# A one-core decode kernel: the second weight of its gated MLP dealt anew over the DMA engines, its first product laid out to match, four fills moved

## The chip, the cores and the metric

The kernel runs on one core of a Trainium2 chip. A core has TensorE (PE), VectorE (DVE), ScalarE (ACT), GpSimd (POOL), SyncE (SP), which here only issues transfers, and sixteen DMA engines that carry every transfer. The metric is the device time of one execution in microseconds. All times inside an execution are counted from the start of the span that the profile shows.

## The reference

Two blocks work on the same four rows (batch 4, one position, 640 columns); their results and the input are added. Block A is attention over a cache, 32 heads of 128 with 4096 positions for each row; block B is a gated MLP whose spatial matrix is 1 x 1.

```python
xn = layernorm(x)                                    # (4, 640)
q  = xn @ wq                                         # (4, 32 heads, 128)
o  = softmax(q @ k_cache^T * 128**-0.5) @ v_cache    # caches: (4, 32, 4096, 128) each
z  = gelu(xn @ w_in)                                 # (4, 1728)
g  = w_sp * layernorm(z[:, 864:]) + b_sp
out = x + o @ wo + (z[:, :864] * g) @ w_out          # w_out: (864, 640)
```

The two caches are 134 MB each in bf16; everything else together is about 14 MB.

## The kernel before, in words

**The stream.** The caches are read in 16 units of keys (K0 to K15) and 16 of values (V0 to V15). A unit is one row of the batch and eight heads, 8.4 MB, with 65,536 bytes for each of the 128 partitions. SP issues every unit (L187) in the order K0, K1, K2, K3, V0, K4, V1, K5 and so on, and at the end the output weight `wo` (L195) in ever smaller parts. The units live in the tile `kv`, five slots of half a unit each. A load is issued only when its two slots are free: K0 goes to slots 3 and 4, K1 to 0 and 1, K2 to 2 and 3, so K2 waits until the first half of K0 has been read, and until block B is done with slot 2.

**A unit of keys.** DVE transposes it in eight steps (L419, into the first part of the tile `w_words`), and PE multiplies each step with the queries (L430). After four units DVE, ACT and POOL do the softmax (L437 to L486), and the next four units of values are multiplied (L501).

**Block B, before the first unit is used.** ACT loads `x` (L120), SP loads `wq` and `w_in` (L126, L129). DVE and POOL normalise `x` (L211 to L228), PE multiplies with `wq` (L299) and with `w_in` (L328), ACT applies gelu (L339, L342), DVE, POOL and ACT do the second layernorm and the gate (L365 to L384), and PE multiplies the result with `w_out` (L397, 52 products into `proj`). Only then may DVE's first transposes begin: `w_out` lies in `w_words`, where the transposed keys go.

**How `w_out` is laid out.** It is held as 128 partitions by 26 columns of 640 numbers. Its 864 rows of 1,280 bytes fill only some partitions, and DVE first fills the tile with zeros (L131). The rows come in pieces; the table `PC` gives for each piece its partitions (first, end, step), first column, number of columns `n`, the number `k` of groups into which the outermost dimension of the source is cut, and the run of rows that one packet takes. Two pieces (`a`, `b`) are issued by SP, four (`w`, `s`, `n`, `l`) by POOL, in that order, all after DVE's fill. A piece does not go over sixteen DMA engines but over few of them:

```python
in_=B_w_out[f_of[t][0]:f_of[t][1], :].rearrange("(r i c) n -> i r (c n)", i=k, c=run)
```

Four further small loads on SP (`marks`, L144) go into a tile that nothing reads.

**Rows of the gate.** The columns of `w_in` follow the rows of `w_out`, so each piece has its own part of the product with `w_in` and its own gelu instructions, which put the results where `w_out` expects them. Before, a piece whose rows are interleaved needs two to six of them.

**Order of the work.** Each engine runs its instructions in the order in which they stand in its queue. A scheduler sets that order for the part ahead of the first unit. On POOL it is: fills and the identities, the four loads of `w_out` (waiting for DVE's fill), `sq` (L217, the squares for the first layernorm), `I4` (L241), the selection matrices, and later block B's gate.

Of the kernel before, what the change touches and what calls it, by code (L numbers as in the profile page):

```python
# [8 lines left out]
ACT = mybir.ActivationFunctionType  # L9
# [3 lines left out]
BF16 = mybir.dt.bfloat16  # L13
# [3 lines left out]
def kernel(  # L17
# [19 lines left out]
    nc = tc.nc  # L37
    P = 128
    B, Sq, D = A_x.shape
    _, H, Sk, Dh = A_k_cache.shape  # L40
    assert Sq == 1 and B == 4 and Dh == P and D % P == 0
    DC = D // P
# [15 lines left out]

    PC = {"w": (0, 28, 2, 0, 9, 7, 9), "a": (32, 52, 1, 0, 10, 5, 10), "n": (68, 92, 2, 0, 8, 6, 8),
          "l": (92, 95, 1, 0, 26, 2, 13), "b": (1, 12, 2, 0, 26, 3, 26), "s": (60, 68, 1, 0, 26, 2, 26)}
    f_of, f_end = {}, 0
    for t, (p0, p1, st, _, n, _, _) in PC.items():
        f_of[t] = (f_end, f_end + len(range(p0, p1, st)) * n)
# [6 lines left out]
    eps = 1e-5  # L72

    const = ctx.enter_context(tc.tile_pool(name="const", bufs=1))
# [12 lines left out]
    def misc_ps(shape, dtype):  # L87
        misc_ctr[0] += 1
        return ps_m.tile(shape, dtype, tag="misc", name=f"misc{misc_ctr[0]}")
# [16 lines left out]
    def at_slot(i, n, off=0):  # L106
        return kv[:, i * SL + off:i * SL + off + n]
# [26 lines left out]
    def load_piece(eng, t):  # L134
        p0, p1, st, c0, n, k, run = PC[t]
        return eng.dma_start(out=w_out[p0:p1:st, c0:c0 + n].rearrange("p c n -> p (c n)"),
                             in_=B_w_out[f_of[t][0]:f_of[t][1], :].rearrange("(r i c) n -> i r (c n)", i=k, c=run))

    load_piece(nc.sync, "a")
    load_piece(nc.sync, "b")  # L140
    marks = const.tile([14, 288], BF16)
    m0 = 0
    for k, m in ((6, 96), (10, 80), (12, 64), (14, 48)):
        nc.sync.dma_start(out=marks[0:k, m0:m0 + m], in_=B_w_out[0:k, 0:m])  # L144
        m0 += m
    sw = load_piece(nc.gpsimd, "w")
    for t in ("s", "n", "l"):
        with tc.issue_after(sw.ins):
            sw = load_piece(nc.gpsimd, t)

# [51 lines left out]
    ident_f = const.tile([P, P], F32)  # L202
    make_identity(nc, ident_f[:])
    ones_f = const.tile([P, P], F32)
    nc.gpsimd.memset(ones_f[:], 1.0)
    eps_t = const.tile([P, 1], F32)
    nc.gpsimd.memset(eps_t[:], eps)

    lnb = ln_t[:XR, D:7 * D].bitcast(F32)
    xf, xc, sq = lnb[:, 0:D], lnb[:, D:2 * D], lnb[:, 2 * D:3 * D]  # L210
# [15 lines left out]
    xnT = const.tile([P, DC, 32], BF16)  # L226
# [17 lines left out]
    i2 = I32[:].rearrange("p (pr c) -> p c pr", c=C2)  # L244
    nc.gpsimd.tensor_tensor(out=SelP[:], in0=i2[:, 0], in1=i2[:, 1], op=ALU.add)
    SelN = const.tile([P, NE, HP * B], F32)
    nc.gpsimd.memset(SelN[:].rearrange("p e x -> p (e x)"), 0.0)
    for q in range(4):
        nc.gpsimd.tensor_scalar(out=SelN[32 * q:32 * q + 32, q % 2], in0=SelP[32 * q:32 * q + 32, :], scalar1=-scale,
                                scalar2=None, op0=ALU.mult)  # L250
# [19 lines left out]
    for q in range(4):  # L270
        nc.gpsimd.tensor_copy(out=SelE[32 * q:32 * q + 32, :, q % 2, :],
                              in_=b8[32 * q:32 * q + 32, 8:8 + HP, None].to_broadcast((32, HP, P // HG)))
# [10 lines left out]
                          in_=ident_f[:].rearrange("p (q x c) -> p q x c", q=2, c=C2))  # L283
# [4 lines left out]
    for hf in range(NH):  # L288
        nc.tensor.matmul(proj[0:32, 0:NO2], lhsT=ident_bf[:XR, 1 - hf:33 - hf],
                         rhs=x_bf[:, hf * NO2:(hf + 1) * NO2], start=(hf == 0), stop=False)  # L290
# [4 lines left out]
    for hf in range(2):  # L295
        for c in range(DC):
            for j in range(NG):
                n0 = j * HG * Dh + hf * 512
                nc.tensor.matmul(q4_ps[32 * j:32 * j + 32, hf * 512:hf * 512 + 512], lhsT=xnT[:, c, :],  # L299
                                 rhs=wq[:, c, n0:n0 + 512], start=(c == 0), stop=(c == DC - 1))  # L300
# [4 lines left out]
    for a in range(2):  # L305
# [9 lines left out]
    w_z = w_in.rearrange("p c (a f) -> p c a f", a=2)  # L315
    zr_ps = [misc_ps([P, 2, 256], F32) for _ in range(2)]


    z_parts = [(0, 0, w_z[:, :, :, f_of["w"][0]:f_of["w"][1]]), (0, 1, w_z[:, :, :, f_of["a"][0]:f_of["a"][1]]),
               (0, 2, w_z[:, :, :, f_of["n"][0]:f_of["l"][1]]), (1, 0, w_z[:, :, :, f_of["b"][0]:f_of["b"][1]])]  # L320
    s_src = w_z[:, :, :, f_of["s"][0]:f_of["s"][1]].rearrange("p d a (r i c) -> p d i a r c", i=2, c=PC["s"][4])
    z_parts += [(1, 1 + i, s_src[:, :, i]) for i in range(2)]
    for c in range(DC):
        for bk, q, src in z_parts:
            w = 1
            for m in src.shape[3:]:
                w *= m
            nc.tensor.matmul(zr_ps[bk][32 * q:32 * q + 32, :, 0:w], lhsT=xnT[:, c, :], rhs=src[:, c],  # L328
                             start=(c == 0), stop=(c == DC - 1))
    z_f = at_slot(2, 2 * 3 * NB, z_at).bitcast(F32).rearrange("p (a n) -> p a n", a=3)  # L330
    z_b = [ppool.tile([P, NB], BF16, tag="p", name=f"z_b{i}") for i in range(2)]
    zT = z_f[:, 0:2, :].rearrange("p a (i j) -> p a i j", j=32)
    nc.gpsimd.memset(z_f[:, 0:2, :], 0.0)
    def gelu(q, bk, f0, c0, n, x, order=None):

        z = zr_ps[bk][32 * q:32 * q + 32, :, f0:f0 + len(range(*x)) * n]
        dst = zT[32 * q:32 * q + 32, :, c0:c0 + n, x[0]:x[1]:x[2]]
        if order is None:
            nc.scalar.activation(out=dst, in_=z.rearrange("p a (x c) -> p a c x", c=n), func=ACT.Gelu_apprx_tanh)  # L339
        else:  # L340
            for a in range(2):
                nc.scalar.activation(out=dst[:, a].rearrange("p c (i r) -> p c i r", i=order),  # L342
                                     in_=z[:, a].rearrange("p (r i c) -> p c i r", i=order, c=n), func=ACT.Gelu_apprx_tanh)

    gelu(0, 0, 0, 0, 9, (0, 28, 2), 7)
    gelu(1, 0, 0, 0, 10, (0, 20, 1), 5)
    gelu(2, 0, 0, 0, 8, (4, 28, 2), 6)
    f_l = f_of["l"][0] - f_of["n"][0]
    for i in range(2):
        for j in range(3):  # L350
            x = 28 + (3 * i + j) // 2
            gelu(2, 0, f_l + 26 * j + 13 * i, 13 * ((3 * i + j) % 2), 13, (x, x + 1, 1))
    gelu(0, 1, 0, 0, 26, (1, 12, 2), 3)
    gelu(1, 1, 0, 0, 26, (28, 32, 1))
    gelu(2, 1, 0, 0, 26, (0, 4, 1))

    one_bf = const.tile([1, P], BF16)
    nc.gpsimd.memset(one_bf[:], 1.0)
    sb_ps = misc_ps([P, 2], F32)
    nc.tensor.matmul(sb_ps[:], lhsT=one_bf[:], rhs=sb_bf[:], start=True, stop=True)  # L360
    sb_f = const.tile([P, 2], F32)
# [30 lines left out]
    for f0 in range(0, FC, 4):  # L392
        for hf in range(NH):
            for fc in range(f0, min(f0 + 4, FC)):
# [3 lines left out]
                                 rhs=w_out[:, fc, hf * NO2:(hf + 1) * NO2],  # L398
                                 start=(fc == 1 and hf == 0), stop=False)
# [158 lines left out]
    for i, item in enumerate(seq):  # L558
# [10 lines left out]
        g, b = divmod(u, B)  # L569
# [22 lines left out]
    for c, hf in ((0, 0), (1, 0), (0, 1), (1, 1), (2, 0), (2, 1)):  # L592
        p = min(c, 1)
# [49 lines left out]
```

## Time and profile before

| what | us |
|---|---|
| median of three runs (663.35 to 663.49) | 663.49 |
| the profiled execution | 663.37 |
| its span | 661.6 |
| DVE busy | 380.1 |
| PE busy (matmul) | 293.2 |
| ACT busy, POOL busy | 75.2, 73.1 |
| bytes moved | 282.60 MB, 427 GB/s over the span |
| POOL issues its four pieces of `w_out` from | 9.84 |
| last piece of `w_out` landed | 39.6 |
| product with `w_in` (L328) from | 25.57 |
| product with `w_out` (L397) from | 44.80 |
| SP issues K2 | 56.03 |

The page of the profile gives busy times and a coarse picture in 40 slices; the chain that ended last says which wait ended last; the timeline gives single instructions. Beside these, the trace has a record for each DMA packet (start, duration, queue, bytes) but not its engine. The engine can be had from them: on a busy engine a packet starts 3 or 4 ns before the one ahead of it ends, so that the records of the first 655 us fall into sixteen chains without a gap. Which chain is which is told by the packets of the pieces and marks, as each piece has its own packet size and its own group of engines. Engines are numbered here 0 to 15 in that way: a piece of SP goes to the first ones (`a` to 0 to 4, `b` to 0 to 2), the four pieces of POOL to 0 to 6, 7 and 8, 9 to 14, and 15. Two engines with the same load can't be told apart.

### The profile page before, as it was taken

How to read it: one execution, taken by the hardware profiler on the slowest of the kernel's cores; microseconds unless marked ns; L12 is line 12 of the kernel's file. 1: busy time of each engine (PE TensorE's matmuls, PEld its weight loads, DVE VectorE, ACT ScalarE, POOL GpSimd, SP SyncE). 2: the span in 40 equal slices, each digit the busy share in tenths (PEclk: the TensorE clock that was granted, in tenths of full speed). 3: DMA queues.
4: the chain of work that ended last, by engine and by line, in shares of the span. 5: the costliest groups of instructions: out<-in, count | busy, mean ns of one | idle time of the engine just before them, and what ended most of it. 6: DMA issues, size and time to landing. Idle time of an engine off the chain costs nothing.

```text
span 661.6 us, 5493 instructions
## 1 busy us (share of the span) xinstructions
PE 293.2 (44%) x2273; PEld 109.6 (17%) x2273; DVE 380.1 (57%) x307; ACT 75.2 (11%) x152; POOL 73.1 (11%) x140
## 2 busy tenths in 40 slices
PE   0436565447063355334426075642607255541236
PEld 0222111112021121111102022210202112120113
DVE  6239989756191758718346196764619175971112
ACT  0310000340100000330200000070100000042200
POOL 5341000030200000130300000030110000002300
PEclk9858878768567686776858578665857758766678
DMA  9999999999999999999999999999999999999997
GB/s 371 463 434 409 429 440 441 440 432 417 432 433 444 437 408 433 440 441 436 429 432 416 445 422 437 442 429 428 440 433 428 437 432 413 456 428 421 431 420 289
DMA packets 7098, 282.60 MB, mean 427 GB/s; under 512 B 1116, under 2 KB 1376, under 8 KB 1632
## 3 DMA queue, kind: packets, MB, share of 16 engines
q1 hardware_dynamic: 6758, 281.60, 98.8%
q0 software_dynamic: 288, 0.65, 0.3%
q8 instruction: 18, 0.29, 0.2%
q14 instruction: 6, 0.05, 0.0%
q10 hardware_dynamic: 28, 0.01, 0.0%
HBM read 282.25 MB, written 0.01 MB: 427 GB/s over the span
## 4 chain that ended last, share of the span: by engine, by line
DMA 71%; DVE 12%; issue 11%; PE 3%; POOL 1%; ACT 1%; SPq 0%; DVEq 0%; POOLq 0%; ACTq 0%
DMA kv<-in_A_k_cache_dram 59%; DVE w_words L419 10%; DMA kv<-in_A_v_cache_dram 5%; DMA kv<-in_B_w_in_dram 4%; DMA kv<-in_A_wo_dram 4%; PE O L501 1%; PE proj L397 1%; POOL kv L381 0%; PE misc L328 0%; DVE w_words L481 0%; DVE w_words L463 0%; PE S L430 0%; POOL z_b L383 0%; ACT kv L342 0%; POOL kv L366 0%
## 5 line engine op out<-in xcount | busy, mean ns | idle before, releaser
L419 DVE STREAM_TRANSPOSE w_words<-kv 128x2048 f32<-128x2048 f32 x128 | 282.9, 2276 | 118.1 <-DMA kv<-in_A_k_cache_dram 115.9
L430 PE MATMUL S<-w_words,QZ 128*32 128x512 bf16 x1024 | 190.6, 506 | 247.2 <-DVE w_words L419 247.1
L430 PEld LDWEIGHTS <-QZ 128*32 128x32 bf16 x1024 | 60.4, 112 | 374.4 <-issue 312.1
L501 PE MATMUL O<-kv,w_words 128*32 128x512 bf16 x1024 | 75.4, 459 | 56.3 <-DMA kv<-in_A_v_cache_dram 45.7
L467 ACT ACTIVATE w_words<-w_words,MkE 32x128 bf16<-32x128 bf16 x120 | 60.9, 508 | 118.0 <-PE O L501 104.9
L510 DVE TENSOR_TENSOR om<-O,Mk 128x512 f32<-128x512 f32 x15 | 10.4, 692 | 95.1 <-PE O L501 95.1
L465 POOL TENSOR_SCALAR w_words<-w_words,MkE 32x128 bf16<-32x128 bf16 x60 | 43.0, 716 | 139.5 <-PE O L501 127.1
L501 PEld LDWEIGHTS <-w_words 128*32 128x32 bf16 x1024 | 34.0, 113 | 97.9 <-issue 69.0
L475 ACT ACTIVATE w_words<-S,negmax 128x1024 bf16<-128x1024 f32 x4 | 4.5, 1114 | 396.3 <-DVE negmax L447 396.3
L463 DVE TENSOR_SCALAR w_words<-w_words,MkE 32x128 bf16<-32x128 bf16 x76 | 24.8, 326 | 2.3
L405 POOL COPY QZ<-qT 32x32 bf16<-32x32 bf16 x16 | 5.1, 316 | 170.4 <-PE S L430 169.8
L511 DVE TENSOR_REDUCE R<-om 128x128 f32<-128x512 f32 x15 | 15.3, 1020 | 0.5
L486 POOL TENSOR_SCALAR rs<-MkB,rowsum 128x4 f32<-128x4 f32 x4 | 1.2, 299 | 112.4 <-ACT w_words L475 112.4
L481 DVE STREAM_TRANSPOSE w_words<-w_words 128x1024 bf16<-128x1024 bf16 (+1 forms) x8 | 9.6, 1241 | 5.6 <-ACT w_words L475 5.6
L534 POOL MEMSET oT<- 128x66 bf16 x4 | 0.5, 156 | 97.9 <-PE proj L544 97.9
L397 PE MATMUL proj<-w_words,z_b 128*8 128x320 bf16 (+1 forms) x52 | 5.6, 394 | 8.8 <-DVE z_b L384 8.8
L131 DVE MEMSET w_words<- 128x8320 f32 x1 | 7.0, 6992 | 2.5 <-issue 2.5
L513 DVE TENSOR_SCALAR R<-O,Mk 128x128 f32<-128x128 f32 x1 | 0.3, 350 | 14.1 <-PE O L501 14.1
L437 DVE TENSOR_REDUCE m<-S 128x1 f32<-128x1024 f32 x4 | 4.9, 1224 | 5.6 <-PE S L430 5.6
L523 PE MATMUL misc<-R,SelX 128*128 128x512 f32 x8 | 4.5, 644 | 7.2 <-DVE R L511 5.5
L299 PE MATMUL q<-kv,xnT 128*32 128x512 bf16 x40 | 4.2, 603 | 6.2 <-DVE xnT L228 6.2
L488 PE MATMUL misc<-rs,SelE 128*128 128x4 f32 x8 | 2.2, 339 | 10.4 <-POOL rs L486 10.4
(100 smaller groups left out, 89.3 us busy)
## 6 DMA issues: line engine op xcount, KB each, us to landing
kv<-in_A_k_cache_dram SPq DMA_DIRECT2D x8, 4096.0 KB
kv<-in_A_v_cache_dram SPq DMA_DIRECT2D x1, 6144.0 KB
kv<-in_A_wq_dram SPq DMA_DIRECT2D x1, 5120.0 KB
kv<-in_A_wo_dram SPq DMA_DIRECT2D x3, 1280.0 KB
kv<-in_B_w_in_dram SPq DMA_DIRECT2D x1, 2160.0 KB, 24.4
kv<-in_A_v_cache_dram SPq DMA_DIRECT2D x1, 2048.0 KB
kv<-in_A_wo_dram SPq DMA_DIRECT2D x1, 640.0 KB
kv<-in_A_wo_dram SPq DMA_DIRECT2D x1, 320.0 KB, 23.9
```

What stands on the lines that cost most here:

```text
L131: nc.vector.memset(w_words[:, 0:FC * NOUT // 2], 0.0)
L397: nc.tensor.matmul(proj[r0:r0 + nb, 0:NO2], lhsT=uT[:, u0:u0 + nb], rhs=w_out[:, fc, hf * NO2:(hf + 1) * NO2], start=(fc == 1 and hf == 0) ...
L405: nc.gpsimd.tensor_copy(out=QZ[r0:r0 + 32, :, :, :, 8 + 8 * hp], in_=qT[32 * g:32 * g + 32, NE * hp:NE * hp + NE].rearrange("p e a b -> p ...
L419: nc.vector.transpose(kT.rearrange("p (t r) -> p t r", r=32), kw)
L430: nc.tensor.matmul(S_ps[32 * q:32 * q + 32, i], lhsT=QZ[:, b, 2 * kh + w, e, w0:w0 + 32], rhs=kb[:, i, :, e, :, w], start=(b == 0 and k < ...
L463: nc.vector.tensor_scalar(out=dst, in0=src, scalar1=mk, scalar2=None, op0=ALU.mult)
L465: nc.gpsimd.tensor_scalar(out=dst, in0=src, scalar1=mk, scalar2=None, op0=ALU.mult)
L467: nc.scalar.activation(out=dst, in_=src, func=ACT.Copy, scale=mk)
L481: nc.vector.transpose(pT_t[:, j0:j1, :], blocks)
L501: nc.tensor.matmul(O_ps[32 * q:32 * q + 32, :, :], lhsT=Zb[b % 2][:, w].rearrange("p h c -> p (h c)"), rhs=vv[:, w * 4 * Dh:(w + 1) * 4 * ...
L510: nc.vector.tensor_tensor(out=om4[:], in0=O_ps[:], in1=Mk4[:, :, None].to_broadcast((P, 4, Dh)), op=ALU.mult)
L511: nc.vector.tensor_reduce(out=R, in_=om4[:].rearrange("p c d -> p d c"), axis=AX.X, op=ALU.add)
```

## The change

`w_out` is cut into seven pieces instead of six. `w`, `a` and `n` have other sizes, `m` is new, and `s` gives three columns of its partitions away. In rows for each engine:

| engines | before | after |
|---|---|---|
| 0, 1, 2 | 110 | 98 |
| 3, 4 | 58 | 46 |
| 5, 6 | 18 | 30 |
| 7, 8 | 104 | 92 |
| 9 to 12 | 16 | 34 |
| 13, 14 | 16 | 10 |
| 15 | 78 | 78 |

POOL now issues five pieces (`w`, `s`, `n`, `m`, `l`), SP two as before, and three marks instead of four, on fewer partitions. The product with `w_in` is cut so that its results lie in the order of the pieces: 70 matmuls instead of 30, with the same columns in all, and then 8 gelu instructions instead of 16. The fills of `ones_f`, `eps_t`, `SelN` and `one_bf` are done by DVE instead of POOL. The scheduler's order changes with it on POOL: `I4` (now L242, which waits for the load of `x`) and `SelP` (L246) now stand ahead of the loads of `w_out` (L137), and `sq` (L218) still stands behind them. On DVE, `ones_f` and `eps_t` stand behind the fill of `w_words`, `SelN` and `one_bf` behind the first step of the layernorm. The product with `w_out` still waits, at its first instruction, for all pieces.

```diff
-    PC = {"w": (0, 28, 2, 0, 9, 7, 9), "a": (32, 52, 1, 0, 10, 5, 10), "n": (68, 92, 2, 0, 8, 6, 8),
-          "l": (92, 95, 1, 0, 26, 2, 13), "b": (1, 12, 2, 0, 26, 3, 26), "s": (60, 68, 1, 0, 26, 2, 26)}
+    PC = {"w": (0, 28, 2, 0, 15, 7, 15), "a": (32, 52, 2, 0, 8, 5, 8), "b": (1, 12, 2, 0, 26, 3, 26),
+          "s": (60, 68, 1, 0, 23, 2, 23), "n": (68, 84, 2, 0, 17, 4, 17), "m": (84, 92, 2, 0, 5, 2, 5),
+          "l": (92, 95, 1, 0, 26, 2, 13)}
...
-    marks = const.tile([14, 288], BF16)
+    marks = const.tile([8, 288], BF16)
...
-    for k, m in ((6, 96), (10, 80), (12, 64), (14, 48)):
+    for k, m in ((2, 96), (4, 80), (8, 64)):
...
-    for t in ("s", "n", "l"):
+    for t in ("s", "n", "m", "l"):
...
-    nc.gpsimd.memset(ones_f[:], 1.0)
+    nc.vector.memset(ones_f[:], 1.0)
...
-    nc.gpsimd.memset(eps_t[:], eps)
+    nc.vector.memset(eps_t[:], eps)
...
-    nc.gpsimd.memset(SelN[:].rearrange("p e x -> p (e x)"), 0.0)
+    nc.vector.memset(SelN[:].rearrange("p e x -> p (e x)"), 0.0)
...
-    z_parts = [(0, 0, w_z[:, :, :, f_of["w"][0]:f_of["w"][1]]), (0, 1, w_z[:, :, :, f_of["a"][0]:f_of["a"][1]]),
-               (0, 2, w_z[:, :, :, f_of["n"][0]:f_of["l"][1]]), (1, 0, w_z[:, :, :, f_of["b"][0]:f_of["b"][1]])]
...
+    z_in = {(0, 0): ('w',), (0, 1): ('a', 's'), (0, 2): ('n', 'm', 'l'), (1, 0): ('b',), (1, 2): ('s',)}
...
+            if x1 - x0 < p1 - p0:
+                parts.append((dst, src[:, :, :, :, (x0 - p0) * k // (p1 - p0)]))
+            elif run < n:
+                d_i = dst.rearrange("p a (i f) -> p i a f", i=k)
+                parts += [(d_i[:, i], src[:, :, :, :, i]) for i in range(k)]
+            else:
+                d_r = dst.rearrange("p a (i r c) -> p r a i c", i=k, c=n)
+                parts += [(d_r[:, r], src[:, :, :, r]) for r in range(m // (k * n))]
...
     for c in range(DC):
-        for bk, q, src in z_parts:
...
+        for parts in z_parts:
+            for j, (dst, src) in enumerate(parts):
+                nc.tensor.matmul(dst, lhsT=xnT[:, c, :], rhs=src[:, c], start=(c == 0 and j == 0),
+                                 stop=(c == DC - 1 and j == len(parts) - 1))
...
-    gelu(0, 0, 0, 0, 9, (0, 28, 2), 7)
-    gelu(1, 0, 0, 0, 10, (0, 20, 1), 5)
-    gelu(2, 0, 0, 0, 8, (4, 28, 2), 6)
...
+    for (bk, q, t), (col, m, n, c0, x0, x1, st) in z_at_col.items():
+        rows = slice(32 * q, 32 * q + 32)
+        nc.scalar.activation(out=zT[rows, :, c0:c0 + n, x0:x1:st],
+                             in_=zr_ps[bk][rows, :, col:col + m].rearrange("p a (x c) -> p a c x", c=n),
+                             func=ACT.Gelu_apprx_tanh)
...
-    nc.gpsimd.memset(one_bf[:], 1.0)
+    nc.vector.memset(one_bf[:], 1.0)
```

More of the change, by code (lines that the diff above doesn't have):

```diff
@@ L316 @@
     zr_ps = [misc_ps([P, 2, 256], F32) for _ in range(2)]
-    z_parts = [(0, 0, w_z[:, :, :, f_of["w"][0]:f_of["w"][1]]), (0, 1, w_z[:, :, :, f_of["a"][0]:f_of["a"][1]]),
-               (0, 2, w_z[:, :, :, f_of["n"][0]:f_of["l"][1]]), (1, 0, w_z[:, :, :, f_of["b"][0]:f_of["b"][1]])]
-    s_src = w_z[:, :, :, f_of["s"][0]:f_of["s"][1]].rearrange("p d a (r i c) -> p d i a r c", i=2, c=PC["s"][4])
-    z_parts += [(1, 1 + i, s_src[:, :, i]) for i in range(2)]
-    for c in range(DC):
-        for bk, q, src in z_parts:
[L325 to L329, printed above, removed]
+    z_in = {(0, 0): ('w',), (0, 1): ('a', 's'), (0, 2): ('n', 'm', 'l'), (1, 0): ('b',), (1, 2): ('s',)}
+    z_at_col, z_parts = {}, []
+    for (bk, q), names in z_in.items():
+        col, parts = 0, []
+        for t in names:
+            p0, p1, st, _, n, k, run = PC[t]
+            x0, x1 = max(p0, 32 * q), min(p1, 32 * q + 32)
+            m = len(range(x0, x1, st)) * n
+            assert col + m <= 256
+            src = w_z[:, :, :, f_of[t][0]:f_of[t][1]].rearrange("p d a (r i c) -> p d a r i c", i=k, c=run)
+            dst = zr_ps[bk][32 * q:32 * q + 32, :, col:col + m]
+            if x1 - x0 < p1 - p0:
[6 more added lines that the diff above has]
+                parts += [(d_r[:, r], src[:, :, :, r]) for r in range(m // (k * n))]
+            z_at_col[bk, q, t] = (col, m, n, PC[t][3], x0 - 32 * q, x1 - 32 * q, st)
+            col += m
+        z_parts.append(parts)
+    for c in range(DC):
+        for parts in z_parts:
+            for j, (dst, src) in enumerate(parts):
+                nc.tensor.matmul(dst, lhsT=xnT[:, c, :], rhs=src[:, c], start=(c == 0 and j == 0),
+                                 stop=(c == DC - 1 and j == len(parts) - 1))
     z_f = at_slot(2, 2 * 3 * NB, z_at).bitcast(F32).rearrange("p (a n) -> p a n", a=3)
@@ L333 @@
     nc.gpsimd.memset(z_f[:, 0:2, :], 0.0)
[L334 to L343, printed above, removed]
-    gelu(0, 0, 0, 0, 9, (0, 28, 2), 7)
-    gelu(1, 0, 0, 0, 10, (0, 20, 1), 5)
-    gelu(2, 0, 0, 0, 8, (4, 28, 2), 6)
[L348 to L355, printed above, removed]
+    for (bk, q, t), (col, m, n, c0, x0, x1, st) in z_at_col.items():
[3 more added lines that the diff above has]
+                             func=ACT.Gelu_apprx_tanh)
     one_bf = const.tile([1, P], BF16)
-    nc.gpsimd.memset(one_bf[:], 1.0)
+    nc.vector.memset(one_bf[:], 1.0)
     sb_ps = misc_ps([P, 2], F32)
```

## The prediction

> **What bounds the kernel now.** I read the page's slices first:
>
> ```profile
> DMA  9999999999999999999999999999999999999997
> GB/s 371 463 434 409 429 440 441 440 432 417 432 433 444 437 408 433 440 441 436 429 432 416 445 422 437 442 429 428 440 433 428 437 432 413 456 428 421 431 420 289
> ```
>
> The sixteen DMA engines are busy from start to end, DVE 57%. The time is the stream's, on its slowest engine. Next the chain that ended last, in order of time:
>
> ```profile
> 1.17 24.36 DMA kv<-in_B_w_in_dram
> ...
> 43.70 1.05 DVE z_b L384
> ...
> 44.80 5.60 PE proj L397 x52
> ...
> 53.61 2.28 DVE w_words L419
> ...
> 56.03 28.28 DMA kv<-in_A_k_cache_dram
> ...
> 633.06 23.63 DMA kv<-in_A_wo_dram
> ...
> 658.74 0.32 DVE o_bf L611
> ```
>
> Block B holds back the first transposes, the fourth of these frees slot 3, and only then is K2 issued (56.03). The chain ends with the last part of `wo`, so what counts is when the slowest engine is done. Third, what the loads of `w_out` wait for and when the product that needs them could run (timeline, DMA view, and the instructions of L397):
>
> ```profile
> 9.84 2.63 POOL L136 DMA_DIRECT2D w_words<-in_B_w_out_dram x4 [5.62 <-DVE w_words L131]
> 10.71 0.48 DVE L211 CAST kv<-kv 8x640 f32<-8x640 bf16 x1 [1.18 <-DMA kv<-in_A_x_dram]
> ```
> ```profile
> q0 software_dynamic: 288, 0.65, 0.3%
> ```
> ```profile
> w_words<-in_B_w_out_dram POOLq DMA_DIRECT2D x1, 97.5 KB, 27.8
> ```
> ```profile
> L397 PEldq EVENT_SEMAPHORE  x3: 51/51/51, 39.6 to 39.8; - x3
> ```
>
> POOL's last piece (`l`) lands 27.8 us after its issue at 11.8, at 39.6, and `z_b` is ready at 44.74: 5.1 us to spare.
>
> The packet records, put into sixteen chains, say the rest. (1) No chain has a gap in 655 us, but one: an engine of 10 and 11 ends K1 at 59.27 and starts K2 at 59.40, while others that end K1 at 59.24 have none. So K2's packets reach the engines 3.2 to 3.4 us after SP's issue, and before has nothing to spare there. (2) The engines end at: 1 to 3, 657.8; 13, 657.5; 0, 657.3; 7 and 8, 657.0 and 657.2; 15, 656.7; 10 or 11, 656.5; 5, 656.3; the others 655.7 to 656.0. The mean is 656.7. (3) 18 packets of 16,384 bytes on the queue "instruction" (PE's code, one each 256 PE instructions) go in turn to engines 13, 14, 5, 6, 9, 10, 11, 12; each puts its engine back by 1.55 us (1.02 to 1.11, and the next packet 0.47 to 0.55 longer). (4) POOL's queue has the same number of items on every engine: 18, which gives the 288. A piece gives each engine as many items as its busiest has packets, and one of 4 bytes that ends it; engines without data get items of 4 bytes. An engine takes one item of POOL's queue, then one of SP's, in turn. `n` landed at 25.7 (11.3 + 14.4) though its own engines were done by 20.8: engines 7 and 8 had to reach its end too. So a piece has landed when the slowest of all sixteen has got to it.
>
> **The re-dealing.** A row costs 1,280 bytes at 27 GB/s, 0.047 us. Twelve rows less on 0 to 4, 7 and 8 is -0.57; +0.57 on 5 and 6; +0.85 on 9 to 12; -0.28 on 13 and 14. Alone this puts the last engine at 657.35 (10 or 11) instead of 657.83: -0.48.
>
> **POOL's order.** `I4` (L242) now waits for `x`, which let DVE go at 10.71, and stands ahead of the loads of `w_out`. With `I4` and `SelP` (14.07 to 14.50 in before) these start at 11.2 to 11.45 instead of 9.84. Before, their first item was taken at 13.87, and an engine free at 13.53 took none; so after, they arrive between 14.8 and 15.5. Queued behind them are `sq` and all that follows: five issues of 0.66 end at 14.6, `sq` starts 1.7 later than at 12.87, `wq`'s product ends at 23.5 instead of 21.8. The wait for `w_in` (25.1 by then) hides that.
>
> **The last piece.** After, an engine has 3 + 5 + 3 + 3 + 7 = 21 items to take. On engine 9, before, the first came at 14.59, ten were gone by 20.6, the three marks and their ends (six small packets of SP) let six pass within 0.1 us, and the last came at 23.03. After, the first comes at 15.22, seven or eight pass between the packets of `w_in` (0.64 each), no mark comes to engine 9, and each of the others waits for a packet of K0 or K1 at 2.42 us. I played this turn-taking through for every engine; for before it gives each engine's last item within 0.03 us. For after the last item of all is at 48.0 to 48.2 (engines 9 to 12), where before it was 39.2. If the items arrive after 15.19, some engine loses another turn: 50.4. Before 14.57: 44.0. 15.1 is the middle, so I take 48.2. With 0.4 until the product sees it (39.2 to 39.6), and 0.2 for its semaphores, L397 starts at 48.85: **+4.05**.
>
> **The product with `w_in` and gelu.** 30 matmuls took 2.72. 70 with the same columns cost nothing more at best, 70 x 0.091 = 6.3 at worst; in their order the ones of one PE quarter follow each other, and I take 4.5. ACT's gelus ran from 29.49 to 32.56. Eight instructions of 0.07 and 1,728 columns at 1.3 ns make 2.8. `z_b` comes at 45.6. The late piece hides this; if it were in time, L397 would start at 45.7, +0.9.
>
> **The four fills** cost DVE at most 0.2 each (0.10 to 0.20 on POOL; w_words' 8,320 columns in 6.99 make 0.11 for 128). Two lie in its idle 1.18 before L211, two add up to 0.4 to the path of `xn`, hidden as above. **One mark less** saves SP 0.36; K0 is issued at 16.6 and needed at 20.6. A fifth piece of POOL costs DVE, PE and ACT nothing by itself.
>
> **K2.** Behind L397 stand K0's products on PE, and DVE's first transpose waits for a part of it; all up to the fourth transpose shifts: K2 is issued at 60.08 and there at 63.3 to 63.45. Engine 14 ends K1 at 59.0, and 5, 6, 9, 12 and one of 10, 11 at 60.0 to 60.1; they stand idle 4.4 and 3.3. 0 to 2, 7, 8 and 15 end it at 63.1 to 64.0. All now start K2 together, and the lead that some engines had for their code packets is gone. From K2's start to the end, an engine with two of them took 596.5 (14: 59.25 to 655.70; 12: 596.54): 63.3 + 596.5 = 659.8. The 18th code packet came at 656.4, its engine done; 80 more PE instructions bring it to about 649.5. It costs nothing, or 1.55 at most; 1.0 is its own duration, and between packets smaller than a unit's I take 1.2. 661.0 against 657.83 is **+3.15**. Later loads have room: V0 +3.0 against 4.6 and V1 +2.0 against 3.45, and their engines run later too.
>
> **Sum.** 663.37 (profiled execution; its span and 1.8 around it) + 3.15 = 666.5; the median lies 0.1 higher, which I leave out. Its own range: 0 to 1.55 for the code packet and 63.2 to 63.45 for K2, 665.2 to 667.0.
>
> **Rivals.** *One turn more* (items after 15.19): L397 at 51.25, K2 2.4 later, 668.9. For it: POOL's first load began 0.3 after its wait, which the order may not hide.
>
> *K2's packets come sooner* than 3.3 after the issue. The load of `wq`, in an idle machine, took 1.0: 61.1 + 596.5 + 1.2 = 658.8, 664.3. Against it: the one gap, and `x`, issued at 1.6 and taken at 5.5. The Trainium skill, "DMA: Bandwidth & Descriptors", "Latency and other measured facts", gives about 0.6 us to the first byte of such a load; by that it would be 663.9 (an estimate). The trace's gap speaks against it here.
>
> *The last piece is in time*, items before 14.57: K2 is there at 60.2, and 60.2 + 596.5 + 1.2 = 657.9 leaves 663.4. For this POOL would have to start at 10.7, before `I4` can be done.
>
> *The turns are not single items*, so that the 21 pass in bunches: no engine waits at K2 and the re-dealing alone is left, 663.37 - 0.48 = 662.9. This is the one that ends on the other side; it decides where the last piece has landed by 44.2 and the product with `w_in` takes no more than its 2.7, so that L397 starts by 44.8. The same title, "Queues, rings and completion order", says that an engine drains a packet of some 9 to 17 descriptors of one ring before it goes to the next; that would give this. Engine 15 speaks against it: 16,640, 65,536, 16,640, 65,536 in strict turn, from 21.0 to 39.2.
>
> **Chances.** Forecast 0.48; one turn more 0.22; K2 sooner 0.09; in time 0.08; re-dealing alone 0.07; something else 0.06, mostly slower. The prediction is 666.5. The range goes from K2 sooner (664.3) to one turn more with its own spread (669.2); left out are in time, re-dealing alone and something else, 0.2. Within 0.2% (1.33 us, about what a measurement of this kernel can tell from no change) lie K2 sooner, in time and re-dealing: 0.24. Slower: forecast, one turn more and most of the rest, 0.74. Faster 0.02.
>
> **What would show it.** Right: 336 packets on queue q0; L242 at 10.7 and POOL's first load at 11.2 to 11.5; the last piece landed at 48.6; L397 from 48.8; K2 issued at 60.1; the DMA row below 9 in the slice around 60; the last `wo` 3 us later. Wrong if POOL's loads start by 10, if L397 starts before 46, or if the engines show no gap at K2.

## The result

The changed kernel takes 669.62 us, median of four runs (668.22 to 672.04); the kernel before, run beside it, 663.49 (663.35 to 663.71). The ratio is 1.0096, 95% interval 1.0066 to 1.0125: slower by about 6 us. The prediction said 666.5 and a range to 669.2: the sign and the place are right, the size is short by 3 us. The profiled execution took 669.65, so against the 663.37 of before 6.28 us have to be explained.

In the changed kernel's page the DMA row and the rate show where the engines stand:

```profile
DMA  9998999999999999999999999999999999999995
GB/s 371 444 437 330 437 409 464 412 429 428 441 436 425 440 417 444 433 441 420 425 440 441 436 412 439 446 429 436 420 441 440 441 428 407 446 425 436 437 412 237
```

The fourth slice (50.1 to 66.8) has 330 GB/s where the kernel before had 409. The same hole by stretches, first of the changed kernel, then of before (after the length come the busy times of PE, its weight loads, DVE, ACT and POOL, then PE's granted clock; the last two columns are the DMA engines' busy share and GB/s):

```profile
59.00:65.20 6.20, 3.42 (x27) 1.10 (x23) 5.92 (x3) 0.00 (x0) 0.21 (x3) 1.00 0.56 201
```
```profile
59.00:65.20 6.20, 3.75 (x23) 1.20 (x22) 5.77 (x4) 0.00 (x0) 0.00 (x0) 0.77 1.08 465
```

The packet records give it engine by engine: K1 ends between 59.08 and 63.98, and no engine has a packet of K2 before 64.90. All sixteen stand idle, for between 0.9 and 6.6 us. What they wait for is in the chain that ended last, in order of time:

```profile
1.55 9.24 DMA kv<-in_A_x_dram
13.98 37.38 DMA w_words<-in_B_w_out_dram
51.72 6.58 PE proj L397 x52
...
637.59 24.80 DMA kv<-in_A_wo_dram
```

Before, this stretch ran through `w_in`, the gate and `z_b`. Now it runs through `x`, the last piece of `w_out` (issued at 13.98, landed 37.38 later) and L397, which starts 6.92 later than in before. Its instructions say the same: the semaphore that ends their wait comes at 51.4, and the matmuls were idle for 17.7 before it because of `w_words`:

```profile
L397 PEldq EVENT_SEMAPHORE  x3: 51/51/51, 51.4 to 51.6; - x3
...
  DMA w_words<-in_B_w_out_dram: 17.7, 1
```

The start of POOL's queue, by its timeline:

```profile
10.85 0.29 POOL L242 COPY kv<-I 128x128 f32<-128x128 f32 x1 [6.89 <-DMA kv<-in_A_x_dram]
11.10 0.45 POOL L246 TENSOR_TENSOR SelP<-I 128x16 f32<-128x16 f32 x1
11.50 3.11 POOL L137 DMA_DIRECT2D w_words<-in_B_w_out_dram  x5
```

`I4` waits for `x`, and the five loads stand behind it, 1.66 later than the four of before. The queue view has the 336 packets, 21 for each engine:

```profile
q0 software_dynamic: 336, 0.81, 0.3%
```

The gate is not to blame. Its product took less than before, not more, and `z_b` is there at 42.78, two microseconds earlier than in before:

```profile
24.90 1.91 PE L345 MATMUL misc<-kv,xnT 128*32 128x210 bf16 x70 [1.21 <-DMA kv<-in_B_w_in_dram]
...
28.09 2.52 ACT L353 ACTIVATE kv<-misc 32x420 f32<-32x420 f32 x8
...
41.74 1.04 DVE L384 STREAM_TRANSPOSE z_b<-z_b 128x832 bf16<-128x832 bf16 x1 [6.52 <-POOL z_b L383]
```

### The profile page after: what moved, and what is told of

It is laid out like the page before. It is cut to its first block, busy times and chain, and to the rows that moved or that the text cites. A ratio compares the mean times of both kernels' runs of the same rounds, so it can differ in the third digit from the quotient of the medians.

```text
span 667.8 us, 5566 instructions
## 1 busy us (share of the span) xinstructions
PE 285.7 (43%) x2313; PEld 109.0 (16%) x2313; DVE 380.3 (57%) x311; ACT 74.7 (11%) x144; POOL 73.5 (11%) x137
## 4 chain that ended last, share of the span: by engine, by line
DMA 70%; issue 14%; DVE 12%; PE 3%; POOL 1%; ACT 0%; DVEq 0%; SPq 0%; ACTq 0%; POOLq 0%
DMA kv<-in_A_k_cache_dram 54%; DVE w_words L419 11%; DMA w_words<-in_B_w_out_dram 6%; DMA kv<-in_A_v_cache_dram 5%; DMA kv<-in_A_wo_dram 4%; PE O L501 1%; DMA kv<-in_A_x_dram 1%; PE proj L397 1%; PE S L430 0%; POOL w_words L137 0%; DVE w_words L481 0%; PE last L544 0%; DVE w_words L463 0%; DVE m L437 0%; ACT w_words L475 0%
## 5 line engine op out<-in xcount | busy, mean ns | idle before, releaser
L430 PE MATMUL S<-w_words,QZ 128*32 128x512 bf16 x1024 | 183.9, 491 | 250.1 <-DVE w_words L419 250.1
L501 PE MATMUL O<-kv,w_words 128*32 128x512 bf16 x1024 | 73.0, 447 | 58.1 <-DMA kv<-in_A_v_cache_dram 51.5
L463 DVE TENSOR_SCALAR w_words<-w_words,MkE 32x128 bf16<-32x128 bf16 x76 | 24.8, 326 | 2.3
L397 PE MATMUL proj<-w_words,z_b 128*8 128x320 bf16 (+1 forms) x52 | 6.6, 445 | 17.7 <-DMA w_words<-in_B_w_out_dram 17.7
L397 PEld LDWEIGHTS <-z_b 128*8 128x8 bf16 (+1 forms) x52 | 3.8, 123 | 20.2 <-issue 17.7
```

The lines of the kernel that those rows point to most:

```text
L397: nc.tensor.matmul(proj[r0:r0 + nb, 0:NO2], lhsT=uT[:, u0:u0 + nb], rhs=w_out[:, fc, hf * NO2:(hf + 1) * NO2], start=(fc == 1 and hf == 0) ...
L430: nc.tensor.matmul(S_ps[32 * q:32 * q + 32, i], lhsT=QZ[:, b, 2 * kh + w, e, w0:w0 + 32], rhs=kb[:, i, :, e, :, w], start=(b == 0 and k < ...
L463: nc.vector.tensor_scalar(out=dst, in0=src, scalar1=mk, scalar2=None, op0=ALU.mult)
L501: nc.tensor.matmul(O_ps[32 * q:32 * q + 32, :, :], lhsT=Zb[b % 2][:, w].rearrange("p h c -> p (h c)"), rhs=vv[:, w * 4 * Dh:(w + 1) * 4 * ...
```

## The experiments

My theory had three links: POOL's loads start late and carry more items, of which each engine takes one for each packet of SP; so the last piece lands late; so L397 and K2 are late, and the engines stand idle. The rivals: the new dealing costs something itself (A), the missing mark (B), the late start by itself (C, F), the fills on DVE (D), slow items for another reason (E), items that slow the stream they pass through (G).

All runs in one table, ordered by the issue of K2. The middle columns are of the profiled execution, of which there is one for each kernel; the last is the median. Each experiment ran beside 21 to 31 runs of the kernel before with a median of 663.42 to 663.56, the changed kernel beside the four above.

| kernel | L397 starts | K2 issued | profiled run | median |
|---|---|---|---|---|
| changed, long marks | 43.38 | 54.96 | 663.16 | 663.23 |
| changed, loads first, long marks | 44.30 | 55.61 | 663.22 | 663.14 |
| before | 44.80 | 56.03 | 663.37 | 663.49 |
| before, fills on DVE | 44.88 | 56.10 | 663.49 | 663.49 |
| changed, six pieces | 44.53 | 56.20 | 663.32 | 663.38 |
| before, long marks | 44.75 | 56.88 | 663.45 | 663.58 |
| changed, loads first | 46.68 | 58.31 | 664.49 | 665.05 |
| changed, fills on POOL | 47.17 | 58.62 | 664.88 | 664.75 |
| loads first, long marks, 4 transpositions | 47.66 | 58.86 | 665.00 | 665.00 |
| changed, old marks | 49.41 | 60.53 | 666.12 | 664.62 |
| before, fills on DVE, 20 items, 3 marks | 50.14 | 61.27 | 665.57 | 665.93 |
| loads first, long marks, 8 transpositions | 51.23 | 63.36 | 669.48 | 669.36 |
| changed | 51.72 | 63.93 | 669.65 | 669.62 |

**Loads first.** `I4` and `SelP` are queued behind POOL's loads.

```diff
+    with tc.issue_after(sw.ins): nc.gpsimd.tensor_copy(out=I4, in_=I32[:, None, :].to_broadcast((P, 4, 32)))
...
+    with tc.issue_after(sw.ins): nc.gpsimd.tensor_tensor(out=SelP[:], in0=i2[:, 0], in1=i2[:, 1], op=ALU.add)
```

> The changed kernel with I4 and SelP queued behind POOL's five loads of w_out. My theory (the loads start late, the last of 21 items lands late, L397 and with it K2 come late and all DMA engines stand idle): first load at 9.9 instead of 11.50, the turns played through give the last item at 44.0, L397 starts at 44.6 instead of 51.72, K2 is issued at about 56, hardly an engine waits for it, and the re-dealing's 0.5 is left: 662.9. Rival A, the re-dealing itself costs the time (engines worse balanced): L397 early, but still 666 or more. Rival B, the missing mark is the cause: L397 stays near 51 and the time at 669.6.

Measured: first load at 9.83, 665.05 (664.36 to 666.50), ratio 1.0028 (1.0018 to 1.0038). 4.6 of the 6.1 us are gone, but not all. Its chain:

```profile
12.30 34.03 DMA w_words<-in_B_w_out_dram
46.68 6.00 PE proj L397 x52
```

L397 still waits for the last piece, 2.1 longer than expected. An engine takes the last item at 45.93; the turns, played through again afterwards, give 44.0 where the items come before 14.2 and 46.5 where they come from 14.3 on, and the first were taken between 13.91 and 14.6. The nine runs lie in two heaps (five at 664.4 to 665.1, four at 666.1 to 666.5). One turn more or less could make them, but only a run of the lower heap was profiled. Rival A was not excluded by this run.

**Fills on POOL.** The four `nc.vector.memset` are `nc.gpsimd.memset` again, nothing else.

> The changed kernel with the four fills back on POOL, nothing else. My theory: the fills matter only through the order of POOL's queue; with them back the loads stand ahead of I4 again, so this is the same as putting the loads first: load at 9.9, last item 44.0, L397 at 44.6, 662.9. If the fills on DVE cost something of their own, this one is faster than the kernel with the loads put first, by up to 0.8. Rival A: 666 or more. Rival B: 669.6.

Measured: 664.75 (664.13 to 666.10), ratio 1.0021 (1.0012 to 1.0030); loads from 9.83, L397 at 47.17. It is what putting the loads first gave, and again short of the 662.9 expected: the fills matter through the order of POOL's queue, as far as a scatter of 2 us can tell. That they have no price of their own is shown below, in the kernel before.

**Old marks.**

```diff
-    for k, m in ((2, 96), (4, 80), (8, 64)):
+    for k, m in ((6, 96), (10, 80), (12, 64), (14, 48)):
```

> The changed kernel with the four old marks (6, 10, 12, 14 packets) in place of three; POOL's loads still start at 11.5. My theory: the turns played through for an arrival at 15.3 give the last item at 49.3 instead of 50.4, so L397 at about 50.5 and some 1.1 less: 668.5. Rival B (the missing mark is the cause): L397 near 45 and 663. Rival A: 669.6, whatever L397 does.

Measured: 664.62 (663.07 to 666.12), ratio 1.0016 (1.0007 to 1.0025), with the loads still at 11.53. A miss: the marks bring 5.0, not 1.1. The profiled run is the slowest of its eleven; in it the last item was taken at 48.63 (49.3 expected) and L397 started at 49.41. The turns were played through for this run nearly right; in the changed kernel the last item came later than played (50.97 for 50.4). In most runs with the old marks it probably came earlier than in the profiled one, to judge by their times; no trace of them shows it. Rival B is not borne out as stated (L397 is at 49 in the profiled run, not at 45), but the small packets of the marks count for more than I had given them: by the medians they alone bring back most of the 6 us.

**The kernel before, its fills on DVE.** The four `nc.gpsimd.memset` are `nc.vector.memset`.

> The kernel before with nothing but the four fills moved to VectorE; POOL's order becomes that of the changed kernel, and its four loads start at 11.5 instead of 9.84. My theory: with 18 items an arrival at 15.3 gives the last item at 42.4 instead of 39.2, still ahead of z_b at 44.74, so L397 stays at 44.8 and the time at 663.5, no change. Rival C, the late start of the loads alone is the price: L397 at 48 or later, 666.5 to 669. Rival D, the fills cost their own time on DVE: 664 to 665 with L397 still released by z_b.

Measured: 663.49 (663.30 to 663.72), ratio 0.9999 (0.9990 to 1.0008). Loads and wait:

```profile
11.10 2.54 POOL L136 DMA_DIRECT2D w_words<-in_B_w_out_dram  x4
```
```profile
L397 PEldq EVENT_SEMAPHORE  x3: 51/51/51, 40.4 to 40.6; - x3
```

With 18 items and four marks the late start moves the last piece from 39.6 to 40.4 (its last item was taken at 39.95, where I had 42.4), and L397 waits for `z_b` at 44.8 as before. Rivals C and D are out.

**Loads first, long marks.** Each mark covers 64 partitions: four packets of 64 bytes on every engine, and one that ends them.

```diff
-    marks = const.tile([8, 288], BF16)
+    marks = const.tile([64, 288], BF16)
...
-    for k, m in ((2, 96), (4, 80), (8, 64)):
+    for k, m in ((64, 32),) * 3:
```

> The changed kernel with the loads put first, as in the first experiment, and its three marks over 64 partitions each (four packets of 64 bytes and one that ends them on every engine, 15 small turns in all). My theory (an item of POOL's queue passes once for each packet of SP's): all 21 items pass between w_in and K0, the turns played through give the last at 24.8 instead of about 46; L397 then waits for z_b only and starts at about 43, K2 is issued at 54 to 54.5, no engine waits for it, and the time is 663.37 - 0.48 = 662.9. Rival A (the re-dealing costs something of its own): L397 at 43 and still 664 or more. Rival E (POOL's items are slow for another reason, as the writing of their descriptors): the last item lands past 40 all the same and the time stays at 664.5 to 666.

Measured: 663.14 (663.07 to 663.39) against 663.56 (663.39 to 663.95), ratio 0.9994 (0.9985 to 1.0003). The last of the 336 items is taken at 24.81 (24.8 expected), and the piece that took 34.0 in the first experiment lands in 13.5:

```profile
w_words<-in_B_w_out_dram POOLq DMA_DIRECT2D x1, 97.5 KB, 13.5
```
```profile
44.30 5.68 PE proj L397 x52
...
55.61 28.30 DMA kv<-in_A_k_cache_dram
```

L397 now waits for `z_b`, K2 follows, and no engine shows a gap there. The last packet of `wo` ends at 657.55, where before has 657.83: the dealing brings 0.28 (0.48 predicted). Rivals A and E are out. It is the fastest kernel of all: none of its eleven runs is slower than any of the 27 runs of before, though the interval of the ratio still reaches 1.

**Long marks alone.** The changed kernel with that second diff only; POOL's loads stay behind `I4`.

> The changed kernel with nothing but the marks widened in the same way; POOL's loads still start at 11.5, behind I4. My theory: fifteen small turns let all items pass by 24.8 however late they come (up to 15.5), L397 at 43 to 43.5 instead of 51.72, no engine waits for K2: 662.9. Rival F (the late start is a price of its own, on top of the turns): between 664 and 668. Rival A: 664 or more. Rival E: 669.6, as before the edit.

Measured: 663.23 (663.13 to 663.46), ratio 0.9995 (0.9987 to 1.0004); first item at 15.15, last at 24.82, L397 at 43.38. The late start has no price of its own (F), and one edit of the marks takes back all of the 6 us.

**The kernel before with a fifth load.** Its dealing and its gelus are untouched; the fills go to DVE, the marks are the three of the changed kernel, and POOL gets one more load into the marks' tile. It was meant to bring three items per engine, 21 in all:

```diff
-    for t in ("s", "n", "l"):
+    for t in ("s", "n", "x", "l"):
...
-            sw = load_piece(nc.gpsimd, t)
+            sw = load_piece(nc.gpsimd, t) if t != "x" else nc.gpsimd.dma_start(out=marks[:, 256:288], in_=B_w_out[0:32, 0:32])
```

> The kernel before with its own dealing of w_out and its own gelus, but the fills on DVE (loads at 11.1 to 11.5), three marks, and a fifth load on POOL's queue ahead of the last piece (32 packets of 64 bytes into the marks' tile, nobody reads them; three items on every engine), so 21 items. My theory: the loss needs neither the new dealing nor the new gelus; the turns played through give the last item at 47.4 (arrival 15.1) to 49.8 (15.5), L397 at 48 to 50.5, K2 issued at 59.5 to 62: 666 to 668. Rival A (the dealing or the gelus are at fault): 663.5 to 664.

Measured: 665.93 (665.57 to 667.21), ratio 1.0039 (1.0026 to 1.0051). From its chain:

```profile
13.72 36.06 DMA w_words<-in_B_w_out_dram
50.14 2.06 PE proj L397 x14
```

The load brought two items per engine, not three: its 64-byte rows were moved in pairs, as 16 packets of 128 bytes, each engine's followed by one that ends it. The queue view has 320 packets, 20 for each engine:

```profile
q0 software_dynamic: 320, 0.65, 0.3%
```

The last item was taken at 49.39. That lies within the 47.4 to 49.8 expected, but by luck: these were played through for 21 items, and with one turn of 2.42 less they would be 45.0 to 47.4 (an estimate). The turns foretell here, as in the changed kernel, a last item that is too early. What the run does show is that L397 comes late without the new dealing and without the new gelus. The time is just below what I expected, and 0.6 below the profiled run with the old marks although K2 is issued 0.74 later. In this kernel the 18th code packet comes at 660.03, when the engines are done; in that one at 654.17, before. That would account for it, but was not tested.

**The kernel before with long marks.** The same widening of its marks.

> The kernel before with three marks over 64 partitions instead of its four. My theory: the last piece lands at about 25 instead of 39.6, but L397 waits for z_b at 44.7 all the same, so nothing changes: 663.4 (663.2 to 663.6). If the wide marks bring something by themselves (K0 issued sooner, one load less), this run shows it: 662.9 or less, and the runs with the changed kernel have to be read against it.

Measured: 663.58 (663.45 to 663.76), ratio 1.0000 (0.9991 to 1.0009). The last item is taken at 25.5 and nothing changes: L397 waits for `z_b`. The marks bring nothing where nobody waits for `w_out`. K2 was issued 0.85 later here than in before (L397 took 6.50 for 5.60), at no cost that the times show. Only one engine starts K2 with no packet right ahead of it, at 60.10; that it is not one of those that end last is likely, but was not shown.

**A late product, `w_out` in time.** The fastest kernel, with `z_b` transposed eight times, or four times, in place of once.

```diff
-    nc.vector.transpose(z_b[1][:], z_b[0][:])
+    for _ in range(8):
+        nc.vector.transpose(z_b[1][:], z_b[0][:])
```

> The kernel with the loads put first and the long marks (all of w_out there by 24.8), with the transposition of z_b done eight times instead of once: DVE is 7.3 us longer at it, and nothing is changed on any DMA queue ahead of K2. It tells apart what a late L397 costs from what late items on POOL's queue cost. My theory (only the lateness of K2 counts): L397 at 51.6 as in the changed kernel, K2 issued between 62.9 and 63.9, its data flow 1.6 to 2.1 later, 597.7 from there to the end of the engine with three code packets, 5.7 behind it: 668 to 669.6. Rival G (the items that wait on POOL's queue slow the stream of K0 and K1): 663.1 to 665.

> The same with four transpositions of z_b instead of one: 3.1 us more. My theory: L397 at 47.4, K2 issued at 58.8 to 59.4, a little later than in the run with the loads put first (58.31, 664.49) and in the one with the fills on POOL (58.62, 664.88), so 664.9 to 665.6. Rival G: 663.1.

Measured with eight: 669.36 (667.40 to 669.90), ratio 1.0081 (1.0067 to 1.0094); with four: 665.00 (663.97 to 665.93), ratio 1.0024 (1.0015 to 1.0033). DVE and SP of the first:

```profile
42.58 8.60 DVE L385 STREAM_TRANSPOSE z_b<-z_b 128x832 bf16<-128x832 bf16 x8 [6.54 <-POOL z_b L383]
```
```profile
63.36 0.33 SPq L188 DMA_DIRECT2D kv<-in_A_k_cache_dram  x1
```

With all of `w_out` there at 25 and K2 issued 0.57 before the changed kernel's, the profiled times differ by 0.17. What POOL's items do to the stream while they wait costs nothing that shows (G); the lateness of L397 is the price. With four the time and the issue of K2 are as expected too.

**Six pieces.** `n` and `m` made one again, so 18 items, with the late start and three marks left as they are.

```diff
-          "s": (60, 68, 1, 0, 23, 2, 23), "n": (68, 84, 2, 0, 17, 4, 17), "m": (84, 92, 2, 0, 5, 2, 5),
+          "s": (60, 68, 1, 0, 23, 2, 23), "n": (68, 92, 2, 0, 13, 6, 13),
...
-    for t in ("s", "n", "m", "l"):
+    for t in ("s", "n", "l"):
...
-    z_in = {(0, 0): ('w',), (0, 1): ('a', 's'), (0, 2): ('n', 'm', 'l'), (1, 0): ('b',), (1, 2): ('s',)}
+    z_in = {(0, 0): ('w',), (0, 1): ('a', 's'), (0, 2): ('n', 'l'), (1, 0): ('b',), (1, 2): ('s',)}
```

> The changed kernel with pieces n and m made one again (twelve partitions of 13 rows on engines 9 to 14, 26 rows on each), so that POOL has four loads and 18 items; its loads still start at 11.5 behind I4, and there are three marks. My theory: with an arrival at 15.5 the turns played through give the last item at 42.4 to 44.3, L397 starts at 43.5 to 45, K2 at 55 to 56.5. Engine 13 has 16 rows more than in the changed kernel (0.75): 663.4 to 664.0. Rival F (the late start is a price of its own): 666 or more. Rival B (the marks alone): 668 or more.

Measured: 663.38 (663.29 to 666.18; two of eleven runs above 664), ratio 1.0006 (0.9997 to 1.0014). The last item was taken at 43.61, L397 started at 44.53. Three items less bring the last piece 7.4 us forward. The 16 rows more on engine 13 cost no more than 0.24 against the fastest kernel by the medians, or 0.38 where each is taken against the runs of before beside it: less than the 0.75 of their transfer.

So the loss needs the late start, the three items of the fifth load and the few marks together: take away any one of them and most or all of it is gone.

## Why the prediction was wrong

- **What bounds it, and where the change acts: right.** POOL's queue, its item-by-item turns, the last piece, L397, K2, idle engines: each link was shown by a run. The changed kernel's engines took one of POOL's items, then one packet of SP's, down to the last item at 50.97. The Trainium skill, "DMA: Bandwidth & Descriptors", "Queues, rings and completion order", has an engine drain a packet of some 9 to 17 descriptors before it changes rings; by that the 21 items would have passed in bunches and nothing been lost. The changed kernel decides against it here, with 4-byte items that each waited for a packet of 65,536 bytes. The runs with long marks fit single turns to within 0.02 (15 small packets of SP's let all items through by 24.8), but bunches would have let them through as well.
- **The step that failed is POOL's order, "they arrive between 14.8 and 15.5", of which I took 15.1.** The loads started at 11.50, outside my 11.2 to 11.45 (`x` let L242 go at 10.85 instead of 10.71, and SelP took 0.45 instead of 0.20), and the first item was taken at 15.48. From the start of the loads to the first item it is 3.9 to 4.0 in every late run (11.10 to 15.11, 11.27 to 15.15, 11.32 to 15.31) and 4.04 in before. Had I added the 4.03 of before to my own 11.2 to 11.45, it would have given 15.2 to 15.5: beyond the 15.19 from which an engine loses a turn. The middle of a range was the wrong choice where a step of 2.42 lies inside it. The rival that I had at 0.22 was the case: L397 at 51.72 where it said 51.25, 669.62 where it said 668.9. Engines 9 to 12, from which I had the 48.0 to 48.2, took their last items at 47.96 to 48.51; the turn was lost on one of the two engines that carry `s` (packets of 29,440 bytes), at 50.97 where the turns gave 50.4. In the profiled execution this puts L397 2.87 later than forecast. That the total comes so near to the rival's is in part luck, as the next two errors nearly cancel.
- **L397 to K2: 12.21, taken as unchanged (11.23).** L397 took 6.58 instead of 5.60; the granted clock was 0.55 during it, 0.65 in before. It went from 0.50 to 1.00 at 57.6, 5.9 after L397's start, and in before at 48.7, 3.9 after it. The length of L397 follows that moment in all the profiles, from 5.26 (3.2 after its start, old marks) up to 6.58. PE's longer wait ahead of it, 17.7 instead of 8.8, is not the reason: the kernel before with long marks waited 8.8 too, and took 6.50. So K2 is issued 7.90 later, not 4.05: 3.85 of the miss, 2.87 from the last piece and 0.98 from this.
- **"K2 issued 60.08 and there at 63.3 to 63.45": the delay of 3.3 was too long for idle engines.** From the issue at 63.93 the first packets are recorded after 0.97 to 1.73, and take 2.6 to 3.4 instead of 2.42. Counted from their ends the data flow 1.6 to 2.1 after the issue. Where most engines are busy, as in the runs with the loads put first and with the fills on POOL, it is 2.6 to 3.8. The Trainium skill's 0.6 for the first byte ("DMA: Bandwidth & Descriptors", "Latency and other measured facts") is nearer to the 0.97 to 1.73 than my row was, and short of it all the same. The shorter delay gave back some 1.3; the rival of sooner packets, at 0.09, had the direction right.
- **From K2's data to the end, 596.5 + 1.2: right in its sum, 597.73** (65.85 to 663.58 on the engine of three code packets). The 18th packet was put at 649.5 because PE has more instructions; it came at 656.9 here, since PE was late too, and at 652.4 in the fastest kernel, against 656.4 in before. Either way it now falls on an engine that still has work.
- **A term that was not in the sum: 0.53 behind the last `wo`.** From its last packet to the end before takes 5.54 and the changed kernel 6.07. PE's clock in this part is 0.61 against 1.00. Together: 3.85 - 1.3 + 0.5 = 3.1, the 669.65 against 666.5.
- **The product with `w_in`, 4.5: too long by more than a factor of two.** It took 1.91, less than before's 2.72. I had bounded it by the number of matmuls alone. The same 70 matmuls took 1.9 with the long marks alone, 2.5 with eight transpositions and 3.0 to 3.3 in five more profiles, so the cut itself is at most worth some 0.6. The difference goes with the granted clock during them: 1.00 where they took 1.9, 0.70 for 2.5, 0.56 and 0.57 for the 3.0 to 3.1 of three profiles. In the two with 3.3 (old marks, four transpositions) a clock of 1.00 is shown, but their traces hold no clock record as early as this, so they say nothing against it. In before the clock was 0.51. Near that clock the cut costs some 0.3 to 0.4; in the changed kernel PE had the full clock instead. Gelu was 2.5 for 2.8. `z_b` came 2.0 earlier instead of 0.9 later. It cost nothing, because the late piece hid it, as the prediction said; with the long marks it is what lets L397 start early.
- **The fills, the mark, the re-dealing.** The fills cost nothing by themselves: right. K0 was issued at 16.68: right. The missing mark was priced at SP's 0.36 alone; its small packets, as turns for POOL's items, are worth up to 5 us together with the widths of the other marks: that price was in the played turns, and too small there. Re-dealing: 0.28 for 0.48.

## What to carry to other kernels

In this kernel a load that shares its DMA engines with a stream of long transfers moved one descriptor for each long one that passed. Where a trace shows such turns, count its descriptors on the busiest engine, multiply by the long packet's time, and compare with the moment when its first reader is ready otherwise. Where that is too late, a few small transfers on the stream's own queue, ahead of the long ones, may let the short load through; here they cost nothing and brought back 6 us. And where a quantised delay has its step inside the range of an input, forecast from the row that fixes the input, not from the middle.

## What the runs showed of the hardware that I had not expected

- The start of a transfer on idle engines: first records 0.97 to 1.73 after the issue, with the first packet stretched to 2.6 to 3.4 from 2.42, so that data flow after 1.6 to 2.1. With the other engines busy it is up to 3.8.
- The clock of the last stretch moved too. In the last stretch of the changed kernel (660.8 to 665.1) the granted clock is 0.61, in before's (655.1 to 658.8) it is 1.00, and a matmul of L544 takes up to 0.47 instead of 0.30. The Trainium skill, "TensorE: Matmul & The Clock Gate", "Part 1: The HAM clock gate (the "warmup" mystery)", says that the gate opens with activity. Here PE had idled 2.51 ahead of this stretch, and 0.85 in before, which would fit; but with the old marks it had idled 2.51 as well, and its matmuls there took 0.30. So the length of the idle time alone does not tell when the clock falls. The traces show a grid: in every profile the stretches of one clock last a multiple of 3.41, but for the last, which the end cuts off. The idle 2.51 lies within one cell of that grid in the changed kernel (658.36 to 661.77, and the clock falls at its end) and over the edge of two with the old marks (at 656.7). With eight transpositions PE idled 2.73 within one cell, and the clock fell as well. That fits, but it is argued from three profiles.
- A late K2 makes a kernel's time spread. The kernels whose K2 is late scatter by 1.6 to 4 us (665.57 to 667.21 with the fifth load, 664.36 to 666.50 with the loads first, 663.07 to 666.12 with the old marks, 668.22 to 672.04 as changed), those whose K2 is in time and whose `w_out` has landed early by 0.3. Turns are not needed for it: with `w_out` there at 25 and only the product late, the times spread by 2.5 (667.40 to 669.90, eight transpositions) and 2.0 (663.97 to 665.93, four). What shifts from run to run was not settled; the moment at which L397 gets its full clock is one candidate, the arrival of POOL's items by some tenths another.
